# An adaptive-norm decode block whose narrow weight rows are taken from the fifth modulation instead of from w2

## The chip, the cores and the metric

The kernel runs on one core of a Trainium2 chip. The metric is the device time of one execution in microseconds (us). Three timed runs of the kernel before gave 697.00, 697.01 and 697.48, median 697.01. The execution that was profiled took 697.47; its span, from the first to the last instruction in the trace, is 695.7, so 1.8 us lie around the span.

## The reference

Two tokens (batch 2, one new position each) go through a block with adaptive layer norm. In short:

```
mod = (silu(c) @ w_mod) -> six rows of 512: sa, ca, ga, sb, cb, gb      # numbered 0 to 5
h = layernorm(x) * (1 + ca) + sa
q = h @ wq                                   # 32 heads of 128
o = softmax(q k^T / sqrt(128)) v             # k, v caches: 2 x 32 x 4096 x 128
x = x + ga * (o @ wo)
h = layernorm(x) * (1 + cb) + sb
x = x + gb * (mish(h @ w1 + b1) @ w2)        # w1: 512 x 1376, w2: 1376 x 512
```

Everything is float32. The caches and weights are about 297 MB, each byte used once. The fifth modulation is gb = silu(c) @ w_mod[:, 2560:3072], a product over 512 rows of weights. Its only use is the factor in the last line.

## The kernel before, in words

**Transfers.** All big inputs are read from memory in an order that `stream()` writes out: 36 rows of pieces, each row landing in one of three SBUF slots (tile `room`, 64 KB on each of 128 partitions). SyncE issues them; a new row may be issued as soon as what it overwrites has been used (`used`, `load`). The last row holds, in this order, m3 and w1 (2400 KB and 1376 KB), then m5 (1024 KB) and w2 in pieces of 1280, 768, 256 and 256 KB. One row earlier stands `w2p`, which fills only 20 partitions (32 to 51) and comes as four transfers of 50 KB.

**Attention.** For every head VectorE multiplies the keys by q and sums (L332, L335), ScalarE takes exponentials, and TensorE (PE) weights the values (`weighted_v`, L373). After the last head come the output projection, the sum xps, and x2 = x + ga * attention.

**The tail, which the change touches.** It is written out by hand, and every engine takes its instructions in the written order.

- The second norm (`centred`, L224 to L232, `rstd`): PE averages over partitions with two products, `mean_b` and `var_b`; VectorE and ScalarE work between them. `busy(n)` (L312) issues products of n x 128 columns by an identity matrix into an unused bank; nothing reads what they compute. There are busy(3), busy(1) and busy(1) in and behind the norm.
- `modulation("3")` (L261): 16 matmuls over the 512 rows of m3. h2t is the normed and modulated row, turned into columns.
- w1 (L528): the 1376 hidden units stand in four groups of PE's output columns, of the widths WIDTHS = (384, 400, 296, 296). The four groups of one step go through the array beside each other.
- The result, one row of 32 partitions for each group, is copied to `hq_pad` (L536 to L538 on ScalarE, L543 on VectorE) and turned into columns by four products with `sel` into `fps` (L548), which was filled with the bias at the start.
- `modulation("5")` (L261), 16 matmuls, then busy(4).
- VectorE and ScalarE compute mish on fps, 30 columns wide (L561 to L568); the result is `actt`. mod[5] is copied (L570).
- w2 (L578): a sum over 15 terms into `yps`, four matmuls each: first five pieces of w2p on 20 partitions (96 rows in all: the remainders of groups 1, 2 and 3 above full chunks of 128), then ten chunks of 128 rows.
- y = yps * mod[5] + x2 (L585, L586), and the store (L587).

A float32 matmul stands in the trace as two records, and as many weight loads (PEld).

Of the kernel before, what the change touches and what calls it, by code (L numbers as in the profile page):

```python
# [11 lines left out]
AX = mybir.AxisListType  # L12

P = 128
WIDTHS = (384, 400, 296, 296)
CHUNKS = [(g, j) for j in range(3) for g in range(4) if WIDTHS[g] >= P * (j + 1)]
ROW0, ROWS, STEP = 32, 20, 4
PIECES = [
    (g, lo, min(ROWS, WIDTHS[g] - lo))
    for g, lo in ((2, 2 * P), (3, 2 * P), (1, 3 * P), (2, 2 * P + ROWS), (3, 2 * P + ROWS))  # L20
]
HEADS = 32
HC = 4
BIG = 8192
W = 2048
HALF = BIG // 2
SIZES = {
    "k": BIG, "v": HALF, "wq": W, "wo": W, "m01": 2 * W, "m2": W, "m3": W, "m4": W, "m5": W,
    "w1": 4 * sum(WIDTHS), "w2": 512 * len(CHUNKS),
    "w2p": 512 * len(PIECES),  # L30
}
OUT_STEP = 1
AHEAD = (14, 22)
# [3 lines left out]
def stream():  # L37


    order, n_v = [], 0  # L40
    for h in range(1, HEADS):
        order.append(("k", h))
        if h % HC == HC - 1 and HC < h < HEADS - 1:
            c = (h + 1) // HC
            order.append([("wq", c), ("wo", c - 2)])
        if h not in AHEAD:
            order += [("v", n_v, 0), ("v", n_v, 1)]
            n_v += 1
# [12 lines left out]
    last = [("v", h, i) for h in range(HEADS - 4, HEADS) for i in range(2)]  # L61
    assert order == [[key] for key in last[:2]], order
    loads += [
        [(last[:2] + [("wo", 6), ("wo", 7), ("m2", 0)], (BIG + 3 * W,))],
        [(last[2:4], (BIG,)), (last[4:6], (BIG,))],
        [([("m4", 0)] + last[6:], (W + HALF, W, W)), ([("w2p", 0)], (512 * len(PIECES),))],
        [
            ([("m3", 0), ("w1", 0)], (W + 2 * sum(WIDTHS), 2 * sum(WIDTHS))),
            ([("m5", 0), ("w2", 0)], (W, 5 * 512, 3 * 512, 512, 512)),
        ],  # L70
    ]
    return loads
# [3 lines left out]
def kernel(  # L76
# [29 lines left out]
    EPS = 1e-5  # L106
    SCALE = DH ** -0.5
    NCH = len(CHUNKS)
    NF = NCH + len(PIECES)

    const = ctx.enter_context(tc.tile_pool(name="const", bufs=1))
    work = ctx.enter_context(tc.tile_pool(name="work", bufs=2))
# [12 lines left out]
    def take(t, keys):  # L125
        lo = 0
        for key in keys:
            kind, n = key[:2]
            part = t[:, lo : lo + SIZES[kind]]
            lo += SIZES[kind]  # L130
            if kind == "k":
                k_t[n] = part.rearrange("p (j d) -> p j d", d=DH)
            elif kind == "v":
                v_t[n, key[2]] = part.rearrange("p (c n) -> p c n", n=512)
            elif kind in ("wq", "wo"):
                (wq_t if kind == "wq" else wo_t)[n] = part.rearrange("p (k n) -> p k n", k=G)
            else:
                w_t[kind] = part.rearrange("p (k n) -> p k n", k={"w2": NCH, "w2p": NF - NCH}.get(kind, G))

    w_t = {}  # L140
    done = set()
# [1 line left out]
    def load(n):  # L143

        t = kvp.tile([P, ROW], F32, tag="room", name=f"room{n}", bufs=3)
        lo = 0
        for keys, srcs in loads[n]:
            take(t[:, lo:], keys)
            for src in srcs:
                dst = t[:, lo : lo + src.shape[-1]]  # L150
                lo += src.shape[-1]
                if src.shape[0] == P:
                    nc.sync.dma_start(out=dst, in_=src)
                    continue
                for i in range(STEP):
                    nc.sync.dma_start(out=dst[ROW0 + i : ROW0 + ROWS : STEP], in_=src[i::STEP])

    loaded = 0

# [14 lines left out]
    nc.gpsimd.memset(cx, 0.0)  # L174
    nc.scalar.dma_start(out=cx[::TB], in_=head)
    cq, xq = cx[:, 0, :], cx[:, 1, :]
    bias = const.tile([P, NF], F32, name="bias")
    nc.scalar.dma_start(out=bias, in_=b1c)
    nc.scalar.preload_act_table_set("natural_log_exp_and_others")
    ident = const.tile([P, P], F32, name="ident")  # L180
    make_identity(nc, ident)
# [23 lines left out]

    ct = const.tile([P, G, R], F32, name="ct")
    h2t = const.tile([P, G, R], F32, name="h2t")
    actt = const.tile([P, NF, R], F32, name="actt")
    for t in (ct, h2t, actt):
        nc.gpsimd.memset(t, 0.0)  # L210
    ov = [psum.tile([P, 512], F32, tag=f"ov{i}", name=f"ov{i}", bufs=1) for i in range(2)]

# [222 lines left out]

    project_q(0)
    project_q(1)
    fps = psum.tile([P, 512], F32, tag="att2", name="fps", bufs=1)[:, : NF * B]
    nc.tensor.matmul(fps, lhsT=ident, rhs=bias[:, :, None].to_broadcast([P, NF, B]), start=True, stop=False, skip_group_check=True)

    used(("m01", 0), ("wq", 0), ("wq", 1))
    for h in range(H):
# [65 lines left out]

    m4 = work.tile([P, P], F32, tag="xn", name="m4", bufs=1)
    nc.scalar.activation(m4, mps4[:, 0, :], AF.Copy, bias=1.0)  # L510
    xc, var, rs = centred(x2, "b", add_x, lambda: busy(3))
    mps3 = modulation("3", 1, wm3)
    busy(1)
    nc.vector.tensor_tensor(out=m4, in0=xc, in1=m4, op=ALU.mult)
    y0, y1 = rstd(var, rs)
    nc.scalar.activation(xc, m4, AF.Copy, scale=y0)
# [1 line left out]
    h2ps = columns(hq, "h2ps")  # L518
    nc.vector.tensor_copy(h2t[:, :, ::TB], h2ps)

    busy(1)
    hq_pad = work.tile([P, 512], F32, tag="o", name="hq_pad")
    nc.gpsimd.memset(hq_pad, 0.0)
    w1ps = wide_ps("w1ps")
    for k in range(G):
        lo = 0
        for g, width in enumerate(WIDTHS):
# [5 lines left out]
                stop=(k == G - 1),  # L533
            )
            lo += width
    nc.scalar.copy(hq_pad[:, : 2 * P], w1ps[:, : 2 * P])  # L536
    nc.scalar.copy(hq_pad[: 2 * R, 2 * P : 3 * P], w1ps[: 2 * R, 2 * P : 3 * P])
    nc.scalar.copy(  # L538
        hq_pad[2 * R :, 2 * P :].rearrange("p (j c) -> p j c", j=2)[:, :, ROW0 : ROW0 + ROWS],
        w1ps[2 * R :, 2 * P : 2 * P + 2 * ROWS].rearrange("p (j c) -> p j c", j=2),  # L540
    )
    g, lo, n = PIECES[2]
    nc.vector.tensor_copy(  # L543
        hq_pad[R * g : R * (g + 1), NJ * P + ROW0 : NJ * P + ROW0 + n], w1ps[R * g : R * (g + 1), lo : lo + n]
    )
    for j in range(NJ + 1):
        g0 = 0 if j < NJ else 1
        nc.tensor.matmul(  # L548
            fps[:, G * B * j : G * B * j + B * (G - g0)],
            lhsT=hq_pad[:, P * j : P * (j + 1)],  # L550
            rhs=sel[:, g0:],
            start=False,
            stop=(j == NJ),
            skip_group_check=True,
        )
    gps = modulation("5", 1, wm5)
    busy(4)
# [33 lines left out]
def _lay_out(np, a):  # L591
# [17 lines left out]
    wm = rows(a["w_mod"])  # L609
    w1 = rows(a["B_w1"])  # L610
    starts = np.cumsum((0,) + WIDTHS)
    b1c = np.zeros((P, len(CHUNKS) + len(PIECES)), a["B_b1"].dtype)
    w2 = np.zeros((P, len(CHUNKS), 512), a["B_w2"].dtype)
    w2p = np.zeros((P, len(PIECES), 512), a["B_w2"].dtype)
    for n, (g, j) in enumerate(CHUNKS):
        f0 = starts[g] + P * j
        b1c[:, n] = a["B_b1"][f0 : f0 + P]
        w2[:, n] = a["B_w2"][f0 : f0 + P]
    for n, (g, lo, rows_n) in enumerate(PIECES):
        f0 = starts[g] + lo  # L620
        b1c[ROW0 : ROW0 + rows_n, len(CHUNKS) + n] = a["B_b1"][f0 : f0 + rows_n]
        w2p[ROW0 : ROW0 + rows_n, n] = a["B_w2"][f0 : f0 + rows_n]

    pieces = {**kv, "wq": wq, "wo": wo, "m01": [wm[:, :, :1024]], "w1": [w1], "w2": [w2], "w2p": [w2p]}
    for n in (2, 3, 4, 5):
# [44 lines left out]
```

## Time and profile before

| | |
|---|---|
| median of three runs | 697.01 us |
| profiled execution | 697.47 us |
| its span | 695.7 us |
| DMA, mean over the span | 428 GB/s |
| busy: PE, VectorE, ScalarE | 282.4, 587.9, 44.1 us |
| granted PE clock, mean | 0.676 |

Nearly the whole span is transfers at a constant rate. VectorE's busy time follows the keys as they arrive. The last 34 us, from 661.9 on, are the tail; there the question for every step is which came last, a transfer or the step before.

### The profile page before, as it was taken

The page shows a single profiled execution, that of the slowest core. Times are in us where ns is not written, and L with a number is a line of the kernel's source. Part 1 is how long each engine was busy: PE and PEld are TensorE (multiplying, and loading weights), DVE is VectorE, ACT ScalarE, POOL GpSimd, SP SyncE. Part 2 cuts the span into 40 slices and gives each one's busy share as a digit, 9 for nine tenths or more (in the row PEclk, how much of TensorE's full clock was granted, in tenths as well). Part 3 has the DMA queues.
Part 4 walks back from the last instruction along what each step waited for, and adds up shares of the span by engine and source line. Part 5 has one row for each costly group of instructions (what it writes and reads, how often), then busy time and mean ns, then how long its engine had stood idle before and what let it go on. Part 6 is the DMA issues. An engine that isn't in the chain of part 4 may idle for free.

```text
span 695.7 us, 3984 instructions
## 1 busy us (share of the span) xinstructions
PE 282.4 (41%) x1668; PEld 104.1 (15%) x1668; DVE 587.9 (85%) x221; ACT 44.1 (6%) x168; POOL 4.4 (1%) x19
## 2 busy tenths in 40 slices
PE   3503334335135615225242805234324426224688
PEld 1200101001001201101110301011101111001236
DVE  3699989999999999999999999999999999899002
ACT  1000000000000000000000000000000000000011
POOL 2000000000000000000000000000000000000000
PEclk9956565668565567666575566557585656666879
DMA  9999999999999999999999999999999999999996
GB/s 387 458 422 422 422 464 437 419 427 426 445 446 422 430 430 434 448 426 423 441 426 448 423 426 433 437 442 430 426 434 438 437 433 427 422 444 419 428 419 285
DMA packets 6986, 297.49 MB, mean 428 GB/s; under 512 B 924, under 2 KB 1060, under 8 KB 1444
## 3 DMA queue, kind: packets, MB, share of 16 engines
q1 hardware_dynamic: 6808, 297.22, 99.0%
q8 instruction: 13, 0.21, 0.1%
q10 hardware_dynamic: 160, 0.02, 0.0%
q14 instruction: 5, 0.04, 0.0%
HBM read 297.16 MB, written 0.07 MB: 427 GB/s over the span
## 4 chain that ended last, share of the span: by engine, by line
DMA 66%; DVE 28%; PE 5%; issue 0%; ACT 0%; SPq 0%; DVEq 0%; ACTq 0%
DMA room<-in_load 66%; DVE room L332 14%; DVE s L335 14%; PE ov L373 2%; PE modps L261 1%; PE qps L305 1%; PE yps L578 1%; PE w1ps L528 0%; PE ov L312 0%; PE otp L396 0%; PE att L404 0%; PE fps L548 0%; DVE m L348 0%; DVE hcw L294 0%; PE hps L251 0%
## 5 line engine op out<-in xcount | busy, mean ns | idle before, releaser
L332 DVE TENSOR_TENSOR room<-room,q 128x8192 f32<-128x8192 f32 x32 | 278.2, 8692 | 46.2 <-DMA room<-in_load 40.4
L335 DVE TENSOR_REDUCE s<-room 128x64 f32<-128x8192 f32 x32 | 277.9, 8684 | 0.4 <-DVE m L348 0.3
L373 PE MATMUL ov<-room,e 128*32 128x512 f32 x1024 | 173.0, 826 | 74.6 <-ACT e L351 50.3
L344 PE MATMUL mt<-d,same 128*128 128x64 f32 x64 | 18.7, 387 | 200.9 <-DVE d L342 200.9
L373 PEld LDWEIGHTS ov<-room,e 128*32 128x32 f32 x1024 | 38.6, 143 | 180.9 <-issue 130.1
L351 ACT ACTIVATE e<-s,m 64x64 f32<-64x64 f32 x64 | 22.1, 345 | 553.5 <-DVE m L348 552.7
L344 PEld LDWEIGHTS mt<-d,same 128*128 128x128 f32 x64 | 13.4, 262 | 229.4 <-DVE d L342 180.7
L305 PE MATMUL qps<-room,hcw 128*128 128x512 f32 x64 | 43.3, 842 | 4.8 <-DMA room<-in_load 4.0
L359 PE MATMUL l<-l,ones 128*128 128x8 f32 x16 | 4.6, 359 | 76.0 <-ACT e L351 76.0
L396 PE MATMUL otp<-pick,o 128*128 128x8 f32 (+2 forms) x72 | 14.0, 322 | 35.7 <-ACT o L388 34.6
L388 DVE COPY o<-ov 128x256 f32<-128x256 f32 x1 | 0.4, 425 | 24.5 <-ACT o L388 24.5
L305 PEld LDWEIGHTS qps<-room,hcw 128*128 128x128 f32 x64 | 17.1, 280 | 26.4 <-issue 20.4
L396 PEld LDWEIGHTS otp<-pick,o 128*128 128x128 f32 x72 | 13.2, 274 | 45.0 <-ACT o L388 44.9
L359 PEld LDWEIGHTS l<-l,ones 128*128 128x128 f32 x16 | 3.8, 296 | 77.4 <-ACT e L351 77.4
L404 PE MATMUL att<-room,ot 128*32 128x512 f32 x62 | 10.8, 750 | 5.6 <-DMA room<-in_load 5.1
L348 DVE TENSOR_REDUCE m<-mt 128x1 f32<-128x64 f32 x32 | 7.0, 218 | 6.8 <-PE mt L344 6.8
L351 ACT ACTIVATION_READ_ACCUMULATOR e<-s,m 64x1 f32 x64 | 11.8, 185 | 0.0
L342 DVE TENSOR_SCALAR d<-half,m 128x64 f32<-128x64 f32 x32 | 8.1, 254 | 1.1
L261 PE MATMUL modps<-room,ct 128*32 128x128 f32 (+1 forms) x160 | 8.1, 346 | 1.2 <-DMA room<-in_load 1.2
L340 DVE TENSOR_REDUCE m<-s 128x1 f32<-128x64 f32 x32 | 7.0, 218 | 0.9
L388 ACT COPY o<-ov 128x512 f32<-128x512 f32 (+1 forms) x9 | 5.1, 562 | 28.0 <-PE ov L373 23.9
L306 ACT ACTIVATE q<-qps 128x512 f32<-128x512 f32 x8 | 4.8, 597 | 14.5 <-PE qps L305 14.4
(104 smaller groups left out, 63.8 us busy)
## 6 DMA issues: line engine op xcount, KB each, us to landing
room<-in_load SPq DMA_DIRECT2D x4, 4096.0 KB, 25.2
room<-in_load SPq DMA_DIRECT2D x1, 7168.0 KB
room<-in_load SPq DMA_DIRECT2D x1, 3072.0 KB, 26.4
room<-in_load SPq DMA_DIRECT2D x3, 1024.0 KB, 28.5
room<-in_load SPq DMA_DIRECT2D x1, 2400.0 KB, 12.4
room<-in_load SPq DMA_DIRECT2D x1, 1376.0 KB, 14.6
room<-in_load SPq DMA_DIRECT2D x1, 1280.0 KB, 15.2
room<-in_load SPq DMA_DIRECT2D x1, 768.0 KB
```

The lines of the kernel that those rows point to most:

```text
L261: nc.tensor.matmul(ps[R * g : R * (g + 1)], lhsT=ct[:, k, :], rhs=t[:, k, :].rearrange("p (m n) -> p m n", m=n)[:, :, P * g : P * (g + 1)] ...
L305: nc.tensor.matmul(ps, lhsT=hcw[:, k, :], rhs=wq_t[ch][:, k, :], start=(k == 0), stop=(k == G - 1))
L332: nc.vector.tensor_tensor(out=k_t[h], in0=k_t[h], in1=qv, op=ALU.mult)
L335: nc.vector.tensor_reduce(out=s_t[h], in_=k_t[h], axis=AX.X, op=ALU.add)
L340: nc.vector.tensor_reduce(out=m_t[h][:, 0:1], in_=s_t[h], axis=AX.X, op=ALU.max)
L342: nc.vector.tensor_scalar(out=d, in0=half, scalar1=m_t[h][:, 0:1], scalar2=None, op0=ALU.mult)
L344: nc.tensor.matmul(mps[h], lhsT=same, rhs=d, start=True, stop=True)
L351: nc.scalar.activation(e_t[i][own_b, :, M * i + 4 * b : M * i + 4 * b + 4], s_t[h][own_b].rearrange("p (c m) -> p c m", m=4), AF.Exp, bias ...
L359: nc.tensor.matmul(lps[n], lhsT=ones, rhs=sum_t[n % 2], start=True, stop=True)
L373: nc.tensor.matmul(ov[bank][R * g : R * (g + 1), :], lhsT=e_t[h % HC][:, NB // 2 * part + c, :], rhs=v_t[h, part][:, c, :], start=(first a ...
L396: nc.tensor.matmul(tps[:, x], lhsT=o_t[m], rhs=pick_t[n][:, m, x], start=(m == 0), stop=(m == 3),)
L404: nc.tensor.matmul(att[R * i : R * (i + 1), :], lhsT=ot_t[n % 2][:, i, :], rhs=wo_t[n][:, i, :], start=(n == 0), stop=(n == H // HC - (2 i ...
```

## The change

The 20-partition pieces no longer hold rows of w2. WIDTHS becomes (384, 384, 352, 256), so w2 has eleven chunks: ten of 128 rows and one of 96 (group 2's last). The first 384 rows of the fifth modulation's weights are three full terms (`m5`, 1536 columns in place of 2048), its next 100 rows are the five pieces on 20 partitions (`m5p`, in the place and the size of w2p), and its last 28 rows stand on partitions 96 to 123 of the slot that holds w2's 96-row chunk. That slot is now the first of w2 and travels with m5 in one transfer of 1024 KB. All transfer sizes in the last rows stay as they were. silu(c) for the 128 rows of the pieces is computed by four small instructions after the last softmax (`ct5`), from columns that come with the bias (12 KB in place of 7.5 KB).

The 20-row terms are issued where busy(3), busy(1) and busy(1) stood; the three full terms and the 28-row term follow behind fps; busy(4) becomes busy(2). w1's result is copied by three ScalarE copies and none on VectorE, fps has three products, mish is 24 columns wide, and w2 has eleven terms.

```diff
-WIDTHS = (384, 400, 296, 296)
+WIDTHS = (384, 384, 352, 256)
...
-            ([("m5", 0), ("w2", 0)], (W, 5 * 512, 3 * 512, 512, 512)),
+            ([("m5", 0), ("w2", 0)], (512 * (M5 + 1), 5 * 512, 3 * 512, 512, 512)),
...
+    gps = ov[1 - N % 2][:, :P]
+    rows5, rest5 = slice(ROW0, ROW0 + ROWS), slice(REST0, REST0 + REST)
+    terms5 = [(ct5[rows5, n, :], w_t["m5p"][rows5, n, :]) for n in range(PIECES)]
+    terms5 += [(ct[:, k, :], wm5[:, k, :]) for k in range(M5)]
+    terms5.append((ct5[rest5, PIECES, :], w2_t[rest5, 0, :]))
+
+    def modulation_5(lo, hi):
+        for n in range(lo, hi):
+            c, w = terms5[n]
+            for g in range(G):
+                nc.tensor.matmul(
+                    gps[R * g : R * (g + 1)], lhsT=c, rhs=w[:, P * g : P * (g + 1)],
+                    start=(n == 0), stop=(n == len(terms5) - 1),
+                )
...
-    xc, var, rs = centred(x2, "b", add_x, lambda: busy(3))
+    xc, var, rs = centred(x2, "b", add_x, lambda: modulation_5(0, 3))
     mps3 = modulation("3", 1, wm3)
-    busy(1)
+    modulation_5(3, 4)
...
-    busy(1)
+    modulation_5(4, PIECES)
...
-    nc.scalar.copy(hq_pad[:, : 2 * P], w1ps[:, : 2 * P])
-    nc.scalar.copy(hq_pad[: 2 * R, 2 * P : 3 * P], w1ps[: 2 * R, 2 * P : 3 * P])
...
-    for j in range(NJ + 1):
...
+    for g in reversed(range(G)):
+        hi = WIDTHS[g]
+        if hi > lo:
+            nc.scalar.copy(hq_pad[: R * (g + 1), lo:hi], w1ps[: R * (g + 1), lo:hi])
+        lo = hi
+    for j in range(NJ):
...
-    gps = modulation("5", 1, wm5)
-    busy(4)
-    f = const.tile([P, 3, NF, B], F32, name="f")
+    modulation_5(PIECES, len(terms5))
+    busy(2)
+    f = const.tile([P, 3, NJ * G, B], F32, name="f")
...
-    for n, (act, w) in enumerate(terms):
+    for n in range(NCH):
+        i = (n - 1) % NCH
+        rows_n = slice(0, REST0 if n == 0 else P)
         for t in range(G):
             nc.tensor.matmul(
                 yps[R * t : R * (t + 1), :P],
-                lhsT=act,
-                rhs=w[:, P * t : P * (t + 1)],
+                lhsT=actt[rows_n, i, :],
+                rhs=w2_t[rows_n, n, P * t : P * (t + 1)],
```

PE's instructions in the norm, before (mean_b and var_b are its two averages, modps the third modulation, ov the products of busy):

```order
L224 MATMUL mean_b<-rs_b,mean_w 128x1
L312 MATMUL ov_108<-e_158,ident 128x256
L312 MATMUL ov_108<-e_158,ident 128x128
L232 MATMUL var_b<-rs_b,mean_w 128x1
L261 MATMUL modps_1417<-room_1337,ct 32x128 x16
L312 MATMUL ov_108<-e_158,ident 128x128
L251 MATMUL h2ps<-ident,hq 128x8
L312 MATMUL ov_108<-e_158,ident 128x128
```

The same stretch of the change; L523 is `modulation_5`, which sums in the bank ov_109:

```order
L226 MATMUL mean_b<-rs_b,mean_w 128x1
L523 MATMUL ov_109<-room_1227,ct_104 32x128 x12
L234 MATMUL var_b<-rs_b,mean_w 128x1
L263 MATMUL modps_1434<-room_1344,ct 32x128 x16
L523 MATMUL ov_109<-room_1227,ct_104 32x128 x4
L253 MATMUL h2ps<-ident,hq 128x8
L523 MATMUL ov_109<-room_1227,ct_104 32x128 x4
```

Twenty matmuls of the five pieces stand where the four products of busy stood; the order of all else is the same.

PE's end, before, from the columns of the hidden row (fps) to the last product (yps):

```order
L548 MATMUL fps<-ident,hq_pad 128x8 x3
L548 MATMUL fps<-ident,hq_pad 128x6
L261 MATMUL modps_1474<-room_1337,ct 32x128 x16
L312 MATMUL ov_108<-e_158,ident 128x256 x2
L578 MATMUL yps<-room_1225,actt 32x128 x20
L578 MATMUL yps<-room_1337,actt 32x128 x40
```

And of the change:

```order
L569 MATMUL fps<-ident,hq_pad 128x8 x3
L523 MATMUL ov_109<-room_1344,ct 32x128 x12
L523 MATMUL ov_109<-room_1344,ct_104 32x128 x4
L314 MATMUL ov_110<-e_160,ident 128x256
L598 MATMUL yps<-room_1344,actt 32x128 x44
```

One of four fps products, one of two busy products and 16 of 60 yps matmuls are gone; the 16 matmuls behind fps stay in number.

## Rows read from the trace of the kernel before

**Rows 1.** The page: shares of the chain that ended last, by engine.

```profile
DMA 66%; DVE 28%; PE 5%; issue 0%; ACT 0%; SPq 0%; DVEq 0%; ACTq 0%
```

**Rows 2.** The chain in order of time: start, length, engine or transfer.

```profile
623.86 38.04 DMA room<-in_load
...
688.84 1.06 PE ov L312 x4
```

**Rows 3.** Transfers by size: KB each, us from issue to landing.

```profile
room<-in_load SPq DMA_DIRECT2D x1, 2400.0 KB, 12.4
...
room<-in_load SPq DMA_DIRECT2D x1, 1024.0 KB, 14.6
...
room<-in_load SPq DMA_DIRECT2D x1, 1280.0 KB, 15.2
...
room<-in_load SPq DMA_DIRECT2D x2, 256.0 KB
...
out<-y SPq DMA_DIRECT2D x1, 64.0 KB, 1.5
```

**Rows 4.** SyncE's timeline: issue of the 2400, 1024, 1280 KB transfers, the store.

```profile
668.12 0.35 SPq L153 DMA_DIRECT2D room<-in_load  x1
...
671.70 0.33 SPq L153 DMA_DIRECT2D room<-in_load  x1
...
674.19 0.33 SPq L153 DMA_DIRECT2D room<-in_load  x1
...
694.16 0.35 SPq L587 DMA_DIRECT2D out<-y  x1
```

**Rows 5.** Stretches: busy us of five engines, granted PE clock, DMA share, GB/s.

```profile
655.00:661.90 6.90, 0.60 (x8) 0.00 (x0) 0.00 (x0) 0.00 (x0) 0.00 (x0) 0.87 0.99 424
661.90:667.00 5.10, 5.06 (x24) 1.18 (x28) 0.00 (x0) 0.00 (x0) 0.00 (x0) 0.50 0.96 411
...
691.40:692.00 0.60, 0.60 (x32) 0.60 (x28) 0.00 (x0) 0.00 (x0) 0.00 (x0) 1.00 0.06 24
692.00:692.20 0.20, 0.20 (x20) 0.20 (x12) 0.00 (x0) 0.00 (x0) 0.00 (x0) 1.00 0.39 82
...
695.20:695.40 0.20, 0.00 (x0) 0.00 (x0) 0.00 (x0) 0.00 (x0) 0.00 (x0) 1.00 0.32 85
```

**Rows 6.** Timeline of the tail: start, length, engine, line, idle time before.

```profile
678.28 0.40 PE L412 MATMUL xps<-room,ot 128*32 128x128 f32 x8
...
679.67 0.90 PE L312 MATMUL ov<-e,ident 128*128 128x256 f32 x4
...
680.39 0.08 DVE L226 DVE_READ_ACCUMULATOR sq_b<-xc_b 128x1 f32 x1
...
680.90 1.08 PE L261 MATMUL modps<-room,ct 128*32 128x128 f32 x32
...
683.35 2.88 PE L528 MATMUL w1ps<-room,h2t 128*32 128x384 f32 x32
...
686.78 1.06 PE L548 MATMUL fps<-ident,hq_pad 128*128 128x8 f32 x8 [0.55 <-ACT hq_pad L536]
686.89 0.19 ACT L538 COPY hq_pad<-w1ps 64x40 f32<-64x40 f32 x1
...
687.76 1.08 PE L261 MATMUL modps<-room,ct 128*32 128x128 f32 x32
...
689.27 0.21 DVE L568 TENSOR_TENSOR actt<-f 128x30 f32<-128x30 f32 x1
...
689.83 1.03 PEld L578 LDWEIGHTS yps<-room,actt 20*32 20x32 f32 x40 [0.33 <-issue]
689.84 3.62 PE L578 MATMUL yps<-room,actt 20*32 20x128 f32 x120
691.06 2.12 PEld L578 LDWEIGHTS yps<-room,actt 128*32 128x32 f32 x80 [0.20 <-issue]
```

**Rows 7.** PE by line and shape, 683 to 687: count, busy us, mean ns.

```profile
L528 PE MATMUL w1ps<-room,h2t 128*32 128x400 f32 x8 | 2.9, 502 | 0.0
```

More of the change, by code (lines that the diff above doesn't have):

```diff
@@ L14 @@
 P = 128
-WIDTHS = (384, 400, 296, 296)
-CHUNKS = [(g, j) for j in range(3) for g in range(4) if WIDTHS[g] >= P * (j + 1)]
+WIDTHS = (384, 384, 352, 256)
+CHUNKS = [(g, j) for j in range(3) for g in range(4) if WIDTHS[g] > P * j]
 ROW0, ROWS, STEP = 32, 20, 4
[L18 to L21, printed above, removed]
+PIECES = 5
+M5 = 3
+REST0 = WIDTHS[2] - 2 * P
+REST = 512 - P * M5 - ROWS * PIECES
 HEADS = 32
@@ L27 @@
 SIZES = {
-    "k": BIG, "v": HALF, "wq": W, "wo": W, "m01": 2 * W, "m2": W, "m3": W, "m4": W, "m5": W,
-    "w1": 4 * sum(WIDTHS), "w2": 512 * len(CHUNKS),
-    "w2p": 512 * len(PIECES),
+    "k": BIG, "v": HALF, "wq": W, "wo": W, "m01": 2 * W, "m2": W, "m3": W, "m4": W, "m5": 512 * M5,
+    "m5p": 512 * PIECES, "w1": 4 * sum(WIDTHS), "w2": 512 * len(CHUNKS),
 }
@@ L65, in stream @@
         [(last[2:4], (BIG,)), (last[4:6], (BIG,))],
-        [([("m4", 0)] + last[6:], (W + HALF, W, W)), ([("w2p", 0)], (512 * len(PIECES),))],
+        [([("m4", 0)] + last[6:], (W + HALF, W, W)), ([("m5p", 0)], (512 * PIECES,))],
         [
             ([("m3", 0), ("w1", 0)], (W + 2 * sum(WIDTHS), 2 * sum(WIDTHS))),
-            ([("m5", 0), ("w2", 0)], (W, 5 * 512, 3 * 512, 512, 512)),
+            ([("m5", 0), ("w2", 0)], (512 * (M5 + 1), 5 * 512, 3 * 512, 512, 512)),
         ],
@@ L108 @@
     NCH = len(CHUNKS)
-    NF = NCH + len(PIECES)
+    NP5 = PIECES + 1
     const = ctx.enter_context(tc.tile_pool(name="const", bufs=1))
@@ L137, in take @@
             else:
-                w_t[kind] = part.rearrange("p (k n) -> p k n", k={"w2": NCH, "w2p": NF - NCH}.get(kind, G))
+                w_t[kind] = part.rearrange("p (k n) -> p k n", k={"w2": NCH, "m5": M5, "m5p": PIECES}.get(kind, G))
     w_t = {}
@@ L150, in load @@
                 dst = t[:, lo : lo + src.shape[-1]]
-                lo += src.shape[-1]
                 if src.shape[0] == P:
                     nc.sync.dma_start(out=dst, in_=src)
-                    continue
-                for i in range(STEP):
-                    nc.sync.dma_start(out=dst[ROW0 + i : ROW0 + ROWS : STEP], in_=src[i::STEP])
+                else:
+                    for i in range(STEP):
+                        nc.sync.dma_start(out=dst[ROW0 + i : ROW0 + ROWS : STEP], in_=src[i::STEP])
+                lo += src.shape[-1]
     loaded = 0
@@ L176 @@
     cq, xq = cx[:, 0, :], cx[:, 1, :]
-    bias = const.tile([P, NF], F32, name="bias")
+    bias = const.tile([P, NJ * G + NP5 * B], F32, name="bias")
     nc.scalar.dma_start(out=bias, in_=b1c)
+    c5 = bias[:, NJ * G :]
+    bias = bias[:, : NJ * G]
     nc.scalar.preload_act_table_set("natural_log_exp_and_others")
@@ L207 @@
     h2t = const.tile([P, G, R], F32, name="h2t")
-    actt = const.tile([P, NF, R], F32, name="actt")
-    for t in (ct, h2t, actt):
+    actt = const.tile([P, NCH, R], F32, name="actt")
+    ct5 = const.tile([P, NP5, R], F32, name="ct5")
+    for t in (ct, h2t, actt, ct5):
         nc.gpsimd.memset(t, 0.0)
@@ L437 @@
     project_q(1)
-    fps = psum.tile([P, 512], F32, tag="att2", name="fps", bufs=1)[:, : NF * B]
-    nc.tensor.matmul(fps, lhsT=ident, rhs=bias[:, :, None].to_broadcast([P, NF, B]), start=True, stop=False, skip_group_check=True)
+    fps = psum.tile([P, 512], F32, tag="att2", name="fps", bufs=1)[:, : NJ * G * B]
+    nc.tensor.matmul(fps, lhsT=ident, rhs=bias[:, :, None].to_broadcast([P, NJ * G, B]), start=True, stop=False, skip_group_check=True)
     used(("m01", 0), ("wq", 0), ("wq", 1))
@@ L475 @@
     denominators(N)
+    sg5 = const.tile([P, NP5 * B], F32, name="sg5")
+    nc.scalar.activation(sg5, c5, AF.Exp, scale=-1.0)
+    nc.vector.tensor_scalar(out=sg5, in0=sg5, scalar1=1.0, scalar2=None, op0=ALU.add)
+    nc.vector.reciprocal(sg5, sg5)
+    nc.vector.tensor_tensor(
+        out=ct5[:, :, ::TB],
+        in0=c5.rearrange("p (n b) -> p n b", b=B),
+        in1=sg5.rearrange("p (n b) -> p n b", b=B),
+        op=ALU.mult,
+    )
     for h in range(H - 3, H - 1):
@@ L500 @@
     w1_t, w2_t = w_t["w1"], w_t["w2"]
+    gps = ov[1 - N % 2][:, :P]
[10 more added lines that the diff above has]
+                    start=(n == 0), stop=(n == len(terms5) - 1),
+                )
     xg = work.tile([P, P], F32, tag="sq", name="xg", bufs=1)
@@ L519 @@
     nc.vector.tensor_copy(h2t[:, :, ::TB], h2ps)
-    busy(1)
+    modulation_5(4, PIECES)
     hq_pad = work.tile([P, 512], F32, tag="o", name="hq_pad")
-    nc.gpsimd.memset(hq_pad, 0.0)
+    nc.gpsimd.memset(hq_pad[:, : NJ * P], 0.0)
     w1ps = wide_ps("w1ps")
@@ L535 @@
             lo += width
-    nc.scalar.copy(hq_pad[:, : 2 * P], w1ps[:, : 2 * P])
-    nc.scalar.copy(hq_pad[: 2 * R, 2 * P : 3 * P], w1ps[: 2 * R, 2 * P : 3 * P])
[L538 to L545, printed above, removed]
-    for j in range(NJ + 1):
-        g0 = 0 if j < NJ else 1
+    lo = 0
+    for g in reversed(range(G)):
[4 more added lines that the diff above has]
+    for j in range(NJ):
         nc.tensor.matmul(
-            fps[:, G * B * j : G * B * j + B * (G - g0)],
+            fps[:, G * B * j : G * B * (j + 1)],
             lhsT=hq_pad[:, P * j : P * (j + 1)],
-            rhs=sel[:, g0:],
+            rhs=sel,
             start=False,
-            stop=(j == NJ),
+            stop=(j == NJ - 1),
             skip_group_check=True,
         )
-    gps = modulation("5", 1, wm5)
-    busy(4)
-    f = const.tile([P, 3, NF, B], F32, name="f")
+    modulation_5(PIECES, len(terms5))
+    busy(2)
+    f = const.tile([P, 3, NJ * G, B], F32, name="f")
     hid = fps.rearrange("p (n b) -> p n b", b=B)
@@ L567 @@
     nc.vector.reciprocal(f[:, 2], f[:, 2])
-    nc.vector.tensor_tensor(out=actt[:, :, ::TB], in0=f[:, 1], in1=f[:, 2], op=ALU.mult)
-    nc.vector.tensor_copy(mod[5], gps[:, 0, :])
+    nc.vector.tensor_tensor(out=actt[:, :, ::TB], in0=f[:, 1, :NCH], in1=f[:, 2, :NCH], op=ALU.mult)
+    nc.vector.tensor_copy(mod[5], gps)
     yps = wide_ps("yps")
-    piece_rows = slice(ROW0, ROW0 + ROWS)
-    terms = [(actt[piece_rows, NCH + n, :], w_t["w2p"][piece_rows, n, :]) for n in range(NF - NCH)]
-    terms += [(actt[:, n, :], w2_t[:, n, :]) for n in range(NCH)]
-    for n, (act, w) in enumerate(terms):
+    for n in range(NCH):
+        i = (n - 1) % NCH
+        rows_n = slice(0, REST0 if n == 0 else P)
         for t in range(G):
@@ L579 @@
                 yps[R * t : R * (t + 1), :P],
-                lhsT=act,
-                rhs=w[:, P * t : P * (t + 1)],
+                lhsT=actt[rows_n, i, :],
+                rhs=w2_t[rows_n, n, P * t : P * (t + 1)],
                 start=(n == 0),
-                stop=(n == NF - 1),
+                stop=(n == NCH - 1),
             )
@@ L611, in _lay_out @@
     starts = np.cumsum((0,) + WIDTHS)
-    b1c = np.zeros((P, len(CHUNKS) + len(PIECES)), a["B_b1"].dtype)
+    b1c = np.zeros((P, 12 + 2 * (PIECES + 1)), a["B_b1"].dtype)
+    m5 = a["w_mod"][:, 512 * 5 :]
+    m5p = np.zeros((P, PIECES, 512), m5.dtype)
+    for n in range(PIECES + 1):
+        f0 = P * M5 + ROWS * n
+        to, size = (ROW0, ROWS) if n < PIECES else (REST0, REST)
+        b1c[to : to + size, 12 + 2 * n : 14 + 2 * n] = a["c"].reshape(2, 512)[:, f0 : f0 + size].T
+        if n < PIECES:
+            m5p[to : to + size, n] = m5[f0 : f0 + size]
     w2 = np.zeros((P, len(CHUNKS), 512), a["B_w2"].dtype)
-    w2p = np.zeros((P, len(PIECES), 512), a["B_w2"].dtype)
     for n, (g, j) in enumerate(CHUNKS):
         f0 = starts[g] + P * j
[L617 to L625, printed above, removed]
+        f1 = min(f0 + P, starts[g + 1])
+        b1c[: f1 - f0, n] = a["B_b1"][f0:f1]
+        w2[: f1 - f0, (n + 1) % len(CHUNKS)] = a["B_w2"][f0:f1]
+    w2[REST0 : REST0 + REST, 0] = m5[512 - REST :]
+    pieces = {**kv, "wq": wq, "wo": wo, "m01": [wm[:, :, :1024]], "w1": [w1], "w2": [w2], "m5p": [m5p], "m5": [rows(m5)[:, :M5]]}
+    for n in (2, 3, 4):
         pieces[f"m{n}"] = [wm[:, :, 512 * n : 512 * (n + 1)]]
@@ L639, in _lay_out @@
             for j, t in enumerate(cuts):
-                arrays[f"load{n}_{i}_{j}"] = np.ascontiguousarray(t[ROW0 : ROW0 + ROWS] if keys == [("w2p", 0)] else t)
+                arrays[f"load{n}_{i}_{j}"] = np.ascontiguousarray(t[ROW0 : ROW0 + ROWS] if keys == [("m5p", 0)] else t)
     return arrays
```

## The prediction

> **What bounds the kernel now.** I read the chain of waits first, then its last part in order of time, then the transfers with their landings, the stretches at the end, and the timeline of the tail. The chain lies on transfers for 66% and on VectorE for 28% [rows 1]; its last wait for a transfer ends at 661.9 [rows 2]. From there it runs over PE and small steps of the other engines to the store. So the chain says that the tail is computing. It says nothing of how far behind the transfers are, and here they are close. The last row's transfers were issued at 668.12, 671.70 and 674.19 and took 12.4, 14.6 and 15.2 us [rows 3, 4]: m3 landed at 680.5, m5 at 686.3, the 1280 KB of w2 at 689.4. Behind that stand another 1280 KB of w2, in 768, 256 and 256 KB, for which no landing is shown; I work it out in two ways.
>
> First: from m5 to the 1280 KB piece the landings are 689.4 - 686.3 = 3.1 us apart. Each landing is that of the part that comes last, and the next 1280 KB in the same order end 3.1 us later: 692.5, the 768 KB at 689.4 + 0.6 x 3.1 = 691.3, the first 256 KB at 691.9. Second: from 691.4 to 692.0 the DMA share is 0.06, one engine of 16, and in the next 0.2 us the last packets pass [rows 5]. The store was issued at 694.16 and landed 1.5 later at 695.66, while its last packets lie in 695.2 to 695.4 [rows 3 to 5]: 0.3 to 0.5 us from the last packet to the landing. That puts w2's end at 692.3 to 692.7. I take 692.5.
>
> [...]
>
> In the kernel before, yps runs from 689.84 to 693.46 [rows 6]. A group of eight records (four matmuls) by itself takes 0.40, as xps at 678.28 does, so the 80 records from 691.06 to 693.46 come every (2.40 - 0.40) / 72 = 0.028, and the last eight start at 693.06. That is about 0.5 us after the last landing. **Half a microsecond is all that PE can gain there.**
>
> **The change part by part.** All against the profiled execution: span 695.7, time 697.47.
>
> *The norm.* busy(3) ran from 679.67 to 680.57, VectorE's last sum ended at 680.47 [rows 6]. Twelve matmuls are 24 records at 0.028, 0.67 us plus about 0.27 until the last is out; var_b comes when both are done. Bounds: 0.1 later, 0.1 earlier (down to VectorE). I take 0. In the other two places four matmuls take 0.40, as xps does [rows 6], where one busy product took much the same, beside VectorE's and ScalarE's steps: 0. Behind each of these stands PE's own next step (m3, h2ps, w1), which waits for VectorE anyway. Two transfers are waited for here: m3 at 680.5, 0.4 before its use at 680.90; and m5p, whose landing no row shows. m5p was issued before m3 on the same queue, so it is there by 680.5 at the worst, when 679.7 is wanted: 0 to 0.8 us. I take 0, since 2400 KB lie between the two; 0.8 would fall under the margin below.
>
> *silu(c) for the pieces.* One ScalarE and three VectorE instructions stand before the values of the last heads; from 655.0 to 661.9 VectorE and ScalarE have no busy time at all [rows 5]: 0. Without that cover it would be four steps of some 0.2, as actt's, 0.8.
>
> *w1.* Eight steps in 2.88, the widest group's record lasting 0.50 [rows 6, 7]: steps of (2.88 - 0.50) / 7 = 0.34. The widest group goes from 400 to 384 columns; in proportion 0.014 a step, 0.11 in all. Bounds 0 (if the sum of the columns, unchanged at 1376, sets the pace) and 0.14. I take 0.1.
>
> *Copies and fps.* Eight records in 686.78 to 687.76, where the next product starts: 0.12 each; six leave 0.25 less. The third copy ended at 687.08 [rows 6], 0.3 after fps began, and four records last 0.5, so the third product doesn't wait. fps ends at 687.84 - 0.25 - 0.1 = 687.5.
>
> *From fps to yps.* VectorE's way from the end of fps (687.84) to the end of actt (689.48) took 1.64, plus 0.06 until PE moves. PE's own way was longer: 16 matmuls, and busy(4) with 1.06 ended last, at 689.90 [rows 2]. With busy(2) it is 1.01 for the 16 matmuls (687.76 to 688.77, 688.84 in the chain), some 0.2 more for the step to 28 rows, 0.53 for busy: 1.74. Both ways end about 1.7 after fps: yps may start at 689.1 or 689.2, 0.7 earlier. Bounds: nothing (the wait for actt unshortened and the row step dear), 0.9.
>
> *yps.* 20 matmuls on 20 partitions took 689.84 to 691.06, 1.22 us; one chunk more costs 8 x 0.028 = 0.22. Removed: 1.0.
>
> *The sum without transfers:* 0.1 + 0.25 + 0.4 (the rest of the 0.7) + 1.0 = 1.75, yps at its end at 691.7. **But the transfers don't move**: the sizes, their order and what releases them stay the same, and 4.5 KB more of bias are 0.01 us at 428 GB/s. yps waits at its second chunk (689.4), at its seventh (691.3) and at its last (692.5). The end is 692.5 + 0.04 + 0.40 = 692.95 in place of 693.46: **0.5 us less**, time 697.47 - 0.5 = 696.97. PE has slack before that: the first ten chunks take 0.40 + 72 x 0.028 = 2.4, less the 0.2 that the last matmuls need to come out, so yps may start as late as 690.3 at no cost, 1.2 after my 689.1.
>
> [...] Where yps goes from 20 to 128 rows, the weight loads pause for 0.20 [rows 6]. [...] The change makes about five such steps more (into and out of the pieces, and to the 28 rows). If all of them lay on the path, 5 x 0.2 = 1.0 would be lost; yps would start at 690.1, still inside the margin, and the forecast would be the same, while the third rival below would shrink to 0.7 of gain.
>
> **The median.** It is 697.01, 0.46 below the profiled execution, with a second run at 697.00 and the third at 697.48. The difference is nearly the half microsecond above. PE's part from 661.9 on depends on its clock (0.50 from 661.9 to 667.0, [rows 5]), and where that rises earlier, PE reaches yps earlier and ends on the last landing even before the change. I read 697.0 as that floor. Then the change takes 0.5 from runs like the profiled one and nothing from the two others.
>
> **The rivals.**
> 1. *The floor of the transfers moves with the run* (the three runs differ in the transfers, not in PE's clock). Then the 0.5 comes off the median: 696.5. For it: transfers fill 695 us, and 0.07% of them is 0.46. Against it: two runs agree within 0.01, as at a floor.
> 2. *The change does nothing at all that can be seen*: m5p late, the steps in the norm dear, yps starting at 690.8. 690.84 + 2.62 = 693.46 is the old end: 697.0 to 697.5. Against it: it takes 1.7 us of losses together.
> 3. *The last pieces are not the floor* (they land by 691.3 in most runs). Then the sum of 1.75 shows: 697.47 - 1.75 = 695.7, or 695.3 off the median. Against it: a DMA engine still works at 691.4 to 692.0 [rows 5].
> 4. *Slower: PE's clock falls in the tail.* [...] The change takes out products of 128 x 128 weights that did nothing but keep PE at work, and adds two waits of some 0.5 us in yps. If the clock fell at w1, PE's terms from there (2.9 + 0.75 + 1.7 + 2.6 = 8.0) would double; 8.0 less the 1.75 gained is 6.2 more: 703.7. It decides once yps starts after 690.8. Against it: the longest wait stays under 1 us, and after the idle 0.55 before fps [rows 6] the clock was still 1.00. [...]
>
> **How the numbers follow.** Forecast (floor at 692.5 in every run) 0.57, 696.97; rival 1 0.22; rival 2 0.08; rival 3 0.09; rival 4 0.04. A measurement of this kernel tells 0.2%, 1.4 us, from no change: faster is under 695.6, slower over 698.4. Rival 3 lies across the lower bound, I give it 0.07 of faster; rival 4 and an unforeseen lateness of the transfers make 0.05 of slower; 0.88 within. The range takes rival 1 with 0.4 of spread below it and rival 2 with 0.2 above: 696.1 to 697.7.
>
> **What would show it.** In the profile of the change: waits of yps for transfers, the last at about 692.5 and a chain that names a transfer just before the end; yps able to start near 689.1; fps with six records ending near 687.5; w1 in 2.8; clock 1.00 from the norm on; the three copies on ScalarE alone. It would be wrong if yps ran without a wait (rival 3), if var_b waited for m5p (rival 2), or if a stretch after 680 showed a clock of 0.50 (rival 4).

## The result: slower by 0.14%

Over 22 runs the change took 698.32 us in the median (696.62 to 699.43), the kernel before 697.29 (696.73 to 698.10) on the same chips: a ratio of 1.0014 with an interval of 1.0007 to 1.0020. The forecast was 696.97 in a range of 696.1 to 697.7, and the change lies outside it, on the slow side.

The 22 times of the change lie in three groups, near 696.7, 698.1 and 699.1. The profile is of an execution of 696.76, at the short end, so it can't show by itself where the microsecond goes. But it shows a thing that the profile before doesn't have. These are the stretches of the tail in the kernel before, beyond those of [rows 5] (length, busy us of PE, PEld, VectorE, ScalarE, GpSimd, then the granted clock):

```profile
678.00:680.00 2.00, 1.69 (x44) 1.40 (x37) 0.74 (x4) 0.36 (x2) 0.08 (x1) 1.00 0.97 411
680.00:682.00 2.00, 1.95 (x39) 1.55 (x37) 1.18 (x7) 0.87 (x3) 0.00 (x0) 1.00 1.02 426
682.00:684.00 2.00, 1.77 (x17) 1.23 (x21) 0.52 (x2) 0.00 (x0) 0.00 (x0) 1.00 1.02 427
684.00:686.00 2.00, 2.00 (x28) 1.14 (x18) 0.00 (x0) 0.00 (x0) 0.00 (x0) 1.00 0.99 414
```

And the same part of the change:

```profile
680.00:682.00 2.00, 1.48 (x41) 1.01 (x41) 0.88 (x4) 0.72 (x3) 0.00 (x0) 1.00 1.05 440
682.00:684.00 2.00, 2.00 (x19) 1.21 (x23) 0.17 (x1) 0.00 (x0) 0.00 (x0) 0.57 1.03 425
684.00:686.00 2.00, 2.00 (x21) 1.27 (x16) 0.00 (x0) 0.00 (x0) 0.00 (x0) 0.58 0.96 399
686.00:688.00 2.00, 1.44 (x16) 0.65 (x7) 0.00 (x0) 0.58 (x3) 0.00 (x0) 1.00 0.99 412
```

PE's clock, 1.00 from 678 on in the profile before, falls to 0.50 from 682.3 to 685.7, behind the norm. The timeline of the change, which answers to [rows 6]:

```profile
678.59 0.86 PE L523 MATMUL ov<-room,ct 20*32 20x128 f32 x24
...
680.34 1.08 PE L263 MATMUL modps<-room,ct 128*32 128x128 f32 x32 [0.52 <-DMA room<-in_load]
...
682.85 4.16 PE L554 MATMUL w1ps<-room,h2t 128*32 128x384 f32 x32
...
687.57 0.83 PE L569 MATMUL fps<-ident,hq_pad 128*128 128x8 f32 x6 [0.56 <-ACT hq_pad L566]
...
689.77 0.20 DVE L589 TENSOR_TENSOR actt<-f 128x22 f32<-128x22 f32 x1
...
690.11 2.64 PE L598 MATMUL yps<-room,actt 96*32 96x128 f32 x88
692.82 0.29 DVE L605 TENSOR_TENSOR y<-yps,mod 128x128 f32<-128x128 f32 x1 [2.67 <-PE yps L598]
```

w1 takes 4.16 in place of 2.88, though its widest group is narrower; fps and yps, behind the fallen stretch, are as short as forecast. yps starts at 690.1, a microsecond later than I had it, and doesn't wait. In this execution that just fits: the end is 0.7 earlier than in the profile before.

A second and a third profile of the change were taken to see a longer execution. A1 in what was expected of them is the theory, tested below, that the first of the three places in the norm decides whether the clock holds.

> The change itself once more, for a second profile: the first is of an execution of 696.76, at the fast end of its 22 times (696.62 to 699.43). Theory A1: if this execution is a slow one (698 to 699.4), the tail shows a longer or a worse placed stretch at a clock of 0.50 than the first profile (682.3 to 685.7), and the steps inside it make up the difference; the transfers land as before. If the transfers made the slow executions: clock as in the first profile, landings 1 to 2 us later.

> As e12, a third profile of the change: theory A1 expects a stretch at 0.50 somewhere between the norm and yps in an execution of 698 or more.

The second took 696.99 and has the same short stretch at a lowered clock as the first (0.58 and 0.57 on the mean of 682 to 684 and 684 to 686, w1 4.11). The third took 697.72. Its stretches:

```profile
678.00:680.00 2.00, 1.67 (x40) 1.14 (x32) 1.35 (x7) 0.28 (x1) 0.00 (x0) 0.95 1.01 428
680.00:682.00 2.00, 2.00 (x34) 1.69 (x34) 0.53 (x3) 0.87 (x3) 0.00 (x0) 0.50 0.99 417
682.00:684.00 2.00, 2.00 (x30) 0.99 (x26) 0.52 (x2) 0.00 (x0) 0.00 (x0) 0.50 1.03 423
684.00:686.00 2.00, 2.00 (x17) 1.32 (x21) 0.00 (x0) 0.00 (x0) 0.00 (x0) 0.50 0.99 410
```

and PE's timeline in it:

```profile
679.84 0.56 PE L234 MATMUL var_b<-rs_b,mean_w 128*128 128x1 f32 x2
680.33 1.93 PE L263 MATMUL modps<-room,ct 128*32 128x128 f32 x32
...
682.80 0.60 PE L253 MATMUL h2ps<-ident,hq 128*128 128x8 f32 x2
...
683.90 4.09 PE L554 MATMUL w1ps<-room,h2t 128*32 128x384 f32 x32
...
691.10 2.61 PE L598 MATMUL yps<-room,actt 96*32 96x128 f32 x88
```

Here the clock is at 0.50 from 679.8 to 686.6, and the third modulation (1.93 in place of 1.08) and h2ps (0.60 in place of 0.39) pay too. yps starts at 691.1, past the 690.8 from which the prediction said that the change loses. 691.10 + 2.61 is 0.25 after the old end of yps (693.46), and the time is 0.25 over the 697.47 of the profile before. Neither the second nor the third reached the 699 that the change often takes; an execution of 699.09 is shown below, of a variant.

### The profile page after: what moved, and what is told of

The parts are those of the page before. It is cut to its first block, busy times and chain, and to the rows that moved or that the text cites. A ratio compares the mean times of both kernels' runs of the same rounds, so it can differ in the third digit from the quotient of the medians.

```text
span 695.0 us, 3978 instructions
## 1 busy us (share of the span) xinstructions
PE 282.6 (41%) x1664; PEld 102.0 (15%) x1664; DVE 588.2 (85%) x223; ACT 44.2 (6%) x169; POOL 4.4 (1%) x20
## 4 chain that ended last, share of the span: by engine, by line
DMA 67%; DVE 28%; PE 4%; issue 0%; ACT 0%; SPq 0%; DVEq 0%; ACTq 0%
DMA room<-in_load 67%; DVE room L334 14%; DVE s L337 14%; PE qps L307 1%; PE ov L375 1%; PE modps L263 1%; PE w1ps L554 1%; PE yps L598 0%; PE ov L523 0%; PE fps L569 0%; DVE m L350 0%; DVE hcw L296 0%; PE ov L314 0%; ACT q L308 0%; SPq L151 0%
## 5 line engine op out<-in xcount | busy, mean ns | idle before, releaser
L308 ACT ACTIVATE q<-qps 128x512 f32<-128x512 f32 x8 | 4.8, 597 | 14.8 <-PE qps L307 14.6
## 6 DMA issues: line engine op xcount, KB each, us to landing
room<-in_load SPq DMA_DIRECT2D x1, 1280.0 KB, 15.1
```

## The experiments

The theories: A, the full 128 x 128 products of busy in the norm held PE's clock up, the 20-row products in their place don't, and the tail loses a stretch to a clock of 0.50. B, the new layout's transfers or w2's new order make it slower. C, the steps between 20-row and 128-row products cost the time; at such a step before yps's 128-row chunks the weight loads pause for 0.20 [rows 6], and the next text calls such steps drains. Later, F: with the clock held, the last transfers set the end, as forecast; P: PE's own order sets it. Each time is a median, with the kernel before on the same chip beside it.

### The 20-row products in the kernel before, and nothing in their place

```diff
-    xc, var, rs = centred(x2, "b", add_x, lambda: busy(3))
+    xc, var, rs = centred(x2, "b", add_x, lambda: thin(0, 3))
...
-    busy(1)
+    thin(3, 4)
...
+                nc.tensor.matmul(
+                    ov[1 - N % 2][R * g : R * (g + 1), :P], lhsT=ct[thin_rows, 0, :],
+                    rhs=w_t["w2p"][thin_rows, n, P * g : P * (g + 1)], start=True, stop=True,
```

> The kernel before, with one part of the change alone: in the norm the busy products (3, 1 and 1 times 128 columns, 128 x 128 weights) are replaced by 20-row products as in the change (12, 4 and 4 matmuls on the pieces of w2p, into an unused bank, nothing reads them); all else, w2 and its order too, is as before. [...] Theory B (the new layout's transfers or w2's new order make the change slower): as before, 697.3. Theory C (the drains between 20-row and 128-row products cost time by themselves): 697.3 to 697.8 at a clock of 1.00 throughout the tail.

Measured: 699.32 (697.88 to 700.92), before 697.44; ratio 1.0028 (1.0017 to 1.0038). Nothing of w2, of the transfers or of the tail's other steps was changed. Two stretches of its profile:

```profile
678.00:680.00 2.00, 1.66 (x36) 1.21 (x28) 1.22 (x7) 0.28 (x1) 0.00 (x0) 0.95 0.92 390
680.00:682.00 2.00, 1.95 (x33) 1.49 (x33) 0.53 (x3) 0.87 (x3) 0.00 (x0) 0.50 1.00 419
```

The next kernel leaves the three busy calls of the norm out:

```diff
-    xc, var, rs = centred(x2, "b", add_x, lambda: busy(3))
+    xc, var, rs = centred(x2, "b", add_x)
...
-    busy(1)
...
-    busy(1)
```

> The kernel before without the busy products in the norm (3, 1 and 1 left out, nothing in their place). Theory A: slower than before, at least as much as with the 20-row products, 698 to 699.5, and a stretch at 0.50 in the tail. Theories B and C: not slower than before, 697.0 to 697.3, since nothing waits for these products.

Measured: 700.02 (699.06 to 700.88), ratio 1.0038 (1.0024 to 1.0052).

```profile
678.00:680.00 2.00, 0.90 (x22) 0.55 (x15) 1.31 (x7) 0.28 (x1) 0.00 (x0) 0.98 0.96 407
680.00:682.00 2.00, 1.98 (x30) 1.87 (x34) 0.61 (x4) 0.87 (x3) 0.00 (x0) 0.50 1.00 421
```

Both lose the clock at the same place, just before 680, and both are a little slower than A expected (698 to 699, and 698 to 699.5). B falls: the old layout is as slow with this one part of the change, and more, since it doesn't have the change's shorter yps (2.6 against 3.6). C falls too: without any 20-row product in the norm it is slowest. Work that nothing reads and that no step waits for is worth 2.6 us here.

### The busy products put back into the change

```diff
-    xc, var, rs = centred(x2, "b", add_x, lambda: modulation_5(0, 3))
+    xc, var, rs = centred(x2, "b", add_x, lambda: (busy(3), modulation_5(0, 3)))
...
+    busy(1)
     modulation_5(3, 4)
...
+    busy(1)
     modulation_5(4, PIECES)
```

> The change with the busy products put back (3, 1, 1) ahead of the 20-row products in the same three places of the norm. It adds PE work of 0.9, 0.3 and 0.3 us; about 0.8 us of it delays the norm, inside the 1.2 us that yps can start later without cost. Theory A: as before or under it, 696.7 to 697.3, clock 1.00 in the tail. Theory B: as the change, 698.3. Theory C: the change plus the delay, 698.5 to 699.

Measured: 696.98 (696.59 to 697.38), before 697.44; ratio 0.9994 (0.9985 to 1.0003). The clock is 1.00 in every stretch of its profile from 678 on, and the longer norm hardly shows in the median. It does in the profiled execution, the longest of its eleven at 697.38: there PE is busy for all of the 2.00 us from 690 to 692 and for 1.29 more behind, so yps shows no wait for a transfer and ends on PE's own order. Then the first place alone:

```diff
-    xc, var, rs = centred(x2, "b", add_x, lambda: modulation_5(0, 3))
+    xc, var, rs = centred(x2, "b", add_x, lambda: (busy(3), modulation_5(0, 3)))
```

> The change with busy(3) put back in the norm's first place alone, ahead of the 12 matmuls on 20 rows; the other two places keep only 20-row products. Theory A1 (the first place, the longest, decides whether PE's clock holds): 696.9 to 697.3, as with all three put back (696.98). Theory A2 (each thin place counts): between the change (698.3) and 697, some 697.5. Theory A3 (the last place, just ahead of w1, decides): 698.

and the other two alone:

```diff
+    busy(1)
     modulation_5(3, 4)
...
+    busy(1)
     modulation_5(4, PIECES)
```

> The change with busy(1) put back in the norm's second and third place, ahead of their four 20-row matmuls; the first place keeps only 20-row products. Theory A1: as the change, 698 to 698.5. Theory A2: some 697.5. Theory A3: 697.

Measured: with the first place alone 696.91 (696.59 to 698.65; before 697.24), with the other two alone 700.39 (699.01 to 701.22). The first place, between the two averages, decides (A1): with it filled the clock is 1.00 in every stretch of the profile from 674 on. But two of the eleven executions took 697.8 and 698.7, and no profile shows why. The second kernel is 2 us slower than the change and than A1 expected: it has more work in front of w1, and in its profile the clock is at 0.50 from 680.3 to 690.6, longer than in any profile of the change. Why it stays low that long is open.

The other fill that the change shortens, behind fps:

```diff
     modulation_5(PIECES, len(terms5))
-    busy(2)
+    busy(4)
```

> The change with busy(4) behind fps as in the kernel before, in place of busy(2); the norm as in the change. In the change's profile the clock falls before w1, ahead of this place. Theory A1 to A3: as the change or up to 0.5 more, 698.3 to 698.8. If the shorter fill behind fps is what lets the clock fall: 697.

Measured: 699.09 (697.44 to 699.66), ratio 1.0024 (1.0015 to 1.0032). It doesn't help; it is 0.3 above what A1 to A3 expected. Its profiled execution, at 699.09, has the change's norm and is as long as the change's longest group:

```profile
679.55 0.38 PE L226 MATMUL mean_b<-rs_b,mean_w 128*128 128x1 f32 x2 [0.31 <-DVE x L533]
...
681.12 1.94 PE L263 MATMUL modps<-room,ct 128*32 128x128 f32 x32
...
684.69 4.25 PE L554 MATMUL w1ps<-room,h2t 128*32 128x384 f32 x32
...
692.47 2.61 PE L598 MATMUL yps<-room,actt 96*32 96x128 f32 x88
```

The norm starts 0.9 later than in the third profile of the change (679.55 against 678.64), and 1.3 later than in the first (678.27), since PE came later from the last values: 32 records of its chain took 6.29 from 661.94 on, and the next 26 began at 671.75; in the first profile of the change the 32 took 5.37 from 661.78 on, and the next 23 began at 669.63. In that profile the clock was at 1.00 from 666 to 682. The profile of the kernel before has such a late start too (679.43), and there the clock was at 0.50 until 667 and again from 670.4 to 673.8. So a part of an execution's time is set ahead of the norm, in a stretch that the two kernels share. Behind the start of the norm the third modulation and most of w1 run at a clock of 0.50 (0.50 on the mean from 682 to 686, 0.57 from 686 to 688). The landings of the transfers are where they were: the 1280 KB piece was issued at 674.18 and took 15.1 us here, 674.03 and 15.1 in the first profile of the change.

### Rows or columns

The 20-row products use 32 columns of weights where busy uses 128. Are the rows or the columns the difference?

```diff
-                    ov[1 - N % 2][R * g : R * (g + 1), :P], lhsT=ct[thin_rows, 0, :],
-                    rhs=w_t["w2p"][thin_rows, n, P * g : P * (g + 1)], start=True, stop=True,
+                    ov[1 - N % 2][R * g : R * (g + 1), :P], lhsT=ct[:, n % G, :],
+                    rhs=w_t["m4"][:, n % G, P * g : P * (g + 1)], start=True, stop=True,
```

> The kernel before with the busy products of the norm replaced by as many products as the pieces need (12, 4 and 4 matmuls of 128 columns), but on 128 rows by 32 columns of weights (m4 by silu(c), into an unused bank, nothing reads them). The kernel with the 20-row products in these places took 699.32. If the number of rows is what counts: as before, 697.4, clock 1.00 in the tail. If the columns of the weights count (32 in place of 128): as with the 20-row products, 699.

Measured: 696.99 (696.64 to 698.23), before 697.24; ratio 0.9998 (0.9989 to 1.0007). Its stretches, against those of the 20-row kernel above:

```profile
678.00:680.00 2.00, 1.64 (x32) 1.19 (x28) 1.13 (x7) 0.28 (x1) 0.00 (x0) 1.00 0.94 399
680.00:682.00 2.00, 1.30 (x40) 1.03 (x40) 0.87 (x4) 0.87 (x3) 0.00 (x0) 1.00 1.00 421
```

The same count of products in the same places, and PE as busy (1.64 and 1.66 us of the two), but the clock holds. The two executions came to the norm differently, though: from 674 to 678 PE was busy for 4.00 us in the 20-row one, for 3.80 here. A closer match is the second profile of the change. From 674 to 678 PE was busy for 3.75 there, from 678 to 680 for 1.67 there and 1.64 here; in both the clock is 1.00 from 674 to 682, and in both PE is idle for a while from 680 to 682 (0.55 us there, 0.44 of it for m3, and 0.70 here). The next stretch, the second profile of the change first, then this kernel:

```profile
682.00:684.00 2.00, 1.93 (x19) 1.23 (x23) 0.19 (x2) 0.00 (x0) 0.00 (x0) 0.58 1.04 433
682.00:684.00 2.00, 1.87 (x28) 1.34 (x32) 0.18 (x2) 0.00 (x0) 0.00 (x0) 1.00 1.03 430
```

With 128 rows under the weights the clock held (1.00), with 20 it didn't (0.58), and the idle time just ahead is in both. How many rows are enough, and whether it is the rows or something that goes with them (the 20-row products also read other tiles), no run tells.

### The pieces elsewhere, and what ends the kernel then

```diff
+    modulation_5(0, 2)
+    xc, var, rs = centred(x2, "b", add_x, lambda: busy(3))
-    xc, var, rs = centred(x2, "b", add_x, lambda: modulation_5(0, 3))
...
-    modulation_5(3, 4)
+    busy(1)
...
-    modulation_5(4, PIECES)
+    modulation_5(2, PIECES)
```

> The change with the busy products back in the norm's first two places (3 and 1) and the 20-row products elsewhere: two pieces ahead of the first average, three ahead of w1. Theory A: 696.7 to 697.1, clock 1.00 in the tail, yps ending on the last transfer. If the narrow products ahead of w1 alone are enough to lower the clock: 698 or more with the stretch at 0.50 behind w1's start. Theory B: 698.3. Theory C: about 698.

Measured: 696.76 (696.53 to 697.10), before 697.44; ratio 0.9992 (0.9983 to 1.0001). It is the quickest of the kernels here that compute the whole output, 1.6 us under the change; against the kernel before the interval just includes no change. PE in its profile:

```profile
679.75 0.35 PE L234 MATMUL var_b<-rs_b,mean_w 128*128 128x1 f32 x2
680.09 1.08 PE L263 MATMUL modps<-room,ct 128*32 128x128 f32 x32
...
682.81 2.77 PE L555 MATMUL w1ps<-room,h2t 128*32 128x384 f32 x32
...
686.14 0.83 PE L570 MATMUL fps<-ident,hq_pad 128*128 128x8 f32 x6 [0.56 <-ACT hq_pad L567]
...
688.68 1.58 PE L599 MATMUL yps<-room,actt 96*32 96x128 f32 x48
690.82 1.08 PE L599 MATMUL yps<-room,actt 128*32 128x128 f32 x32 [0.56 <-DMA room<-in_load]
692.10 0.42 PE L599 MATMUL yps<-room,actt 128*32 128x128 f32 x8 [0.20 <-DMA room<-in_load]
```

This is the tail as the prediction drew it: w1 in 2.8, six records in fps, yps waiting for its seventh chunk and again for its last, and eight records behind the last landing. Its chain names the transfer:

```profile
675.45 16.60 DMA room<-in_load
692.05 0.04 issue
692.10 0.47 PE yps L599 x8
```

It also prices the low clock. From the start of var_b to that of yps it took 8.93 (679.75 to 688.68), the third profile of the change 11.26 (679.84 to 691.10). The difference of 2.33 is the third modulation (1.93 - 1.08 = 0.85), h2ps (0.21) and w1 (4.09 - 2.77 = 1.32), 2.38 in sum.

Two more test whether the transfers really set that end (e5 in their texts is this kernel):

```diff
-    busy(2)
+    busy(6)
```

> The kernel of e5 (696.76) with busy(6) behind fps in place of busy(2): PE reaches yps 1.0 us later. Theory F: costs nothing, 696.7 to 696.9, since yps waits that long for its last transfer. Theory P: 697.7.

```diff
-    for n in range(NCH):
+    for n in range(NCH - 2):
```

> The kernel of e5 (696.76) with the last two chunks of w2 left out of yps: 256 rows of w2 don't enter the output, their transfers are still made, nothing waits for them. Theory F (with the clock held, the end is set by the last transfers): the last wait is for the 768 KB piece, which came 1.3 us before the last one; 24 records behind it instead of 8 take 0.45 more, so 0.8 less: 695.9. Theory P (PE's own order sets the end): 16 records less, 0.45: 696.3.

Measured: with a microsecond more of PE's work ahead of yps 696.78 (696.55 to 697.91), the same as without; in its profile yps starts at 689.65 and waits once, for the last landing, until 692.11. Without the last two chunks 696.0 (695.81 to 696.51), 0.76 less, of the 0.8 that F expected against 0.45. F fits both, though the second profile is of an execution in which PE came late (yps at 689.79) and ended on its own order, so for that kernel the transfer's part is read from the times alone.

## Why the prediction was wrong

**The step that failed** is the first term of the sum: the norm. I costed the exchange of busy for the 20-row products at 0, with bounds of 0.1 to either side, because I compared how long each keeps PE and who waits behind it. Both were right: the 24 records took 0.86 against 0.90, and var_b was not late. What the exchange cost was the clock of the steps behind it: 1.4 us of w1 in the first profile (4.16 against 2.77), most of which fell into PE's slack, and 2.4 us over the norm and w1 in the third profile, which didn't. The bounds had no room for that, since they were bounds on the place itself.

**Rival 4 is what happened**, and I gave it 0.04. Its mechanism was named, with the sentence that the removed products do nothing but keep PE at work. The argument against it was about waits: none over a microsecond, and the clock still up after 0.55 of idling. That was the wrong question. I compared busy times, and the clock fell behind 1.66 us of busy PE in 2 in one kernel and held behind 1.64 in another. What narrow products do in a gap the kernel before could not show, since its twenty 20-row matmuls stood at the very end. But its trace has a fall of the clock ahead of the norm.

```profile
667.00:670.40 3.40, 2.43 (x24) 1.27 (x20) 0.00 (x0) 0.75 (x2) 0.00 (x0) 1.00 0.98 410
670.40:673.80 3.40, 3.40 (x20) 0.93 (x16) 0.00 (x0) 0.59 (x1) 0.00 (x0) 0.50 1.07 452
```

PE's waits there were of 0.71 and 0.26 us. The first profile of the change has waits of 0.72 and 0.26 at the same steps and stays at 1.00, so waits this short were followed by a fall in one execution and not in the other. The price of 6.2 us, from doubling everything behind w1, was too high, because the clock came back before fps (at 685.7 and 686.6 in two profiles of the change); the measured loss is 1.0 in the median. No run shows the doubling either: in the third profile the third modulation, all of it at 0.50, took 1.93 against 1.08, and w1 4.09 against 2.77. The threshold (yps after 690.8) was right.

**The floor of the transfers** was right as a mechanism and half a microsecond late in the profile where it shows: landings that released PE at 690.82 and 692.10 where I had 691.3 and 692.5. The last packets pass earlier there, none of them behind 692.0 (0 GB/s from 692 to 694), where in the profile before one of w2's queue still passes. So the floor moves a little with the execution, as rival 1 had it. One reading on the way was wrong: nearly all that passes from 692.0 to 692.2 in [rows 5] is a single packet of 0.02 MB on the instruction queue, and not w2; it changes the estimate by 0.1. The forecast of 696.97 is about what the change does where the clock holds: 696.98, 696.91 and 696.76 in three variants. That the first is so close is luck, since its profiled execution ends on PE's own order.

**The other terms**: w1 0.1 (2.88 to 2.77), fps 0.25 (1.06 to 0.83), fps to yps 1.7 (686.97 to 688.68), yps 1.0 (3.62 to 2.64), and the slack of PE, a microsecond of which cost nothing. m5p was never waited for. m3 was, for 0.52 in the first profile; PE reached it earlier than in [rows 6], and the wait lay inside PE's slack, since yps in that execution started at 690.11, before 690.3.

**The median**: reading 697.0 as a floor was too simple. The kernel before goes down to 696.7 in the later series, close to the 696.76 of the moved pieces, but its median lies 0.5 to 0.7 above; in its one profile PE was last.

## What to carry to other kernels

Work that nothing waits for and nothing reads can still keep a clock up (without it 700.02 here, with it 697.44): before replacing it, ask not only how long the replacement keeps the engine but whether it is the same kind of work, and price every step that comes behind at the lower clock. If a gap has to be filled, try products on many rows there, which held the clock here (696.99), and the narrow ones elsewhere, where they cost nothing (696.76). And look at more than one execution: the first profile showed a gain of 0.7 us for a change that loses 1.0.

## What was not expected of the hardware

- With products on 20 rows by 32 columns in the gap between two averages PE's clock fell to 0.50 behind it, with products on 128 rows by 32 columns it stayed at 1.00, at 1.66 and 1.64 us of busy time in the same two microseconds; medians 699.32 and 696.99.
- One gap of 0.9 us decided it. With its 128 x 128 products back the change took 696.91, with only the later two gaps filled 700.39.
- The transfers' end hardly moves: the 1280 KB piece took 15.2 us from issue to landing in the profile before, 15.1 in two executions 2.3 us apart in time, and 14.8 with the pieces moved. Where yps waited for the last landing, it released PE at 692.10 and 692.11 in two kernels.
